# A linear-attention layer and a GELU MLP on one core: the state sums of four chunks accumulated in PSUM, and the second group's units planned ahead of the weights

## The chip, the cores and the metric

The kernel runs on 1 core of one Trainium2 chip. The time is the device time of one execution, in microseconds (us); before the change it is 546.49 us, the median of 3 runs (546.25 to 547.72). A core has TensorE (PE, matrix products), VectorE (DVE), ScalarE (ACT), GpSimd (POOL), and SyncE (SP), which here issues most transfers. Each engine works through its own list of instructions in order, and they wait for each other by semaphores. TensorE writes its results to PSUM, in banks, and VectorE and ScalarE read them there.

## The reference

```python
def _attn_ref(q, k, v, alpha):                # batch 4, heads 8, seq 768, head_dim 48
    state = np.zeros((B, H, D, D))
    for t in range(S):
        state = alpha[:, :, t, :, None] * state + np.einsum('bhd,bhe->bhde', k[:, :, t], v[:, :, t])
        y[:, :, t] = np.einsum('bhd,bhde->bhe', q[:, :, t], state)
    return y

def _moe_ref(x, w_in, w_out):                 # x 3072x384, w_in 384x2048, w_out 2048x384, float64 weights
    h = x @ w_in
    g = 0.5 * h * (1.0 + erf(h / sqrt(2)))
    return g @ w_out
```

A recurrence with a decay per channel gives y; y, with its heads laid side by side, goes through a two-layer MLP with an exact GELU.

## The kernel before

**Units.** The sequence of each batch is cut into 3 groups of 256 steps, so there are 12 groups (g = 0 to 11), and a group's 8 heads are two units of four heads (u = 0, 1): 24 units, numbered 2g + u. A unit has four chunks of 64 steps (j = 0 to 3). For a unit VectorE makes running products of the decay forward (`forward`, L251) and backward (`backward`, L262) and scales q and k with them. So within a unit the state is a plain sum of k v over the chunks, with no decay left between them.

A unit then passes TensorE three times. `scores` and `turned` (L281, L290) make the products of q and k within each chunk and a transposed k; ScalarE copies the latter (`turned_out`, L297) and VectorE masks the former (`masked`, L302). `inside` multiplies the masked scores with v (L319) and, chunk by chunk, k with v (L337): the state sum of each chunk, each in its own columns of the PSUM tile `ybank`. `chain` (L354, L356) turns these into the states ahead of chunks 1 to 3 and behind chunk 3 by four VectorE instructions, each of which adds one chunk's sum to the state before. `outside_part` (L381) multiplies q with those states and adds to the same `ybank`. `carry` (L361) rescales the last state for the next group of the same batch. Then `x_high` and `x_low` (L423, L427) split y into two parts, and after unit u = 1 `spread` (L436) moves six pieces of 16 rows so that x fills 128 partitions. A check of the decay's range on ScalarE (L162) decides at the end whether a general path has to redo the work; with these inputs it does not run.

**MLP.** Each f32 product is made from parts of high and low precision: `gemm1` (L444) is 18 matmuls for a slice f of 256 hidden features (f = 0 to 7) and one group, `gelus` (L455, L456) and `gelu_low` (L461) make the two parts of the GELU, `gemm2` (L472) is 12 matmuls into an accumulator. I call the two products of one (g, f) a step: 96 steps.

**Weights.** They arrive as 64-bit numbers in 16 pieces (a to p), two for a slice f. Each is fetched by SP and turned into a high and a low part by five VectorE instructions (L198, L202, L212, L217, L227), two ScalarE ones and one more on VectorE (L233).

**What sets the order.** A planner in the program places the operations of all engines by their costs (`COST`), their dependences and a rank; the result is written out in that order by hand and fixed for TensorE, VectorE, ScalarE and SP. `ORDER` gives the ranks of the first units (digits) and of the pieces (letters). A step (g, f) needs slice f's pieces and group g's x; until all pieces are there only groups 0 to 2 may have steps. Some buffers are single: the masked scores, the transposed k and the PSUM tiles `s` and `ybank`, so one unit's `inside` waits for the unit before.

**Tile shapes.** A matmul on 64 rows and 64 columns of operands takes a quarter of TensorE's array, and the program gives each its shape and place in it: L281, L319, L337 and L381 have 64x64 (rows x columns), L290, L444 and L472 128x128.

**Start.** `pads` (L104, L106) fills rows of the operand buffers that no load writes.

Of the kernel before, what the change touches and what calls it, by code (L numbers as in the profile page):

```python
# [8 lines left out]
F32 = mybir.dt.float32  # L9
# [6 lines left out]
ALU = mybir.AluOpType  # L16
# [7 lines left out]
WAIT = 0.15  # L24
SLOW = 1.8
COST = dict(
    scan=2.25, back=2.05, q=1.35, scores=1.2, kn=0.6, mask=0.62, inside=1.2, chain=1.15, outer=0.85, carry=0.26,
    xh=0.6, xl=0.65, spread=2.0, check=0.95, load=2.6, fetch=0.4, u=0.92, c0=0.56, c1=0.9, c2=0.56, c3=0.95, c4=0.92,
    hi=0.84, lo=0.9, gemm1=2.12, gelu=0.58, low=0.63, gemm2=2.1, part=1.1,
)  # L30
ORDER = "0 1 a b c d 2 e 3 f g 4 h i 5 j k l m n o p"


@with_exitstack
def gla_then_gelu_ffn(ctx: ExitStack, tc: tile.TileContext, q, k, v, alpha, qg, kg, ag, w_in, w_out, out):
    nc = tc.nc
    B, H, D, S = q.shape
    NF, P, NK, _ = w_in.shape
    DM, DFF = NK * P, NF * P
    NT = B * S  # L40
    C = 128
    G = 2 * C
    CS = C // 2
    NCH = G // CS
    DP = 64
    NPAIR = H // 2
    NU = NPAIR // 2
    DR = DP - D
    NF2 = NF // 2
    GPB = S // G  # L50
# [6 lines left out]
    const = ctx.enter_context(tc.tile_pool(name="const", bufs=1))  # L57
# [41 lines left out]
    def pads(i, n, p0, p1, eng):  # L99
        for r0 in (DP // 2, DP + DP // 2):  # L100
            r = slice(r0, r0 + DP // 2)
            t = data[i][n][r, p0:p1].rearrange("p a t -> p (a t)")
            if eng is nc.scalar:
                eng.copy(t, (ones if n == "a" else zero)[r].to_broadcast(t.shape))  # L104
            else:
                eng.memset(t, 1.0 if n == "a" else 0.0)  # L106

    for n in "akq":
        pads(0, n, 0, 1, nc.vector)
    for n, eng in (("a", nc.gpsimd), ("k", nc.scalar), ("q", nc.vector)):  # L110
        pads(0, n, 1, NPAIR, eng)
    for n, eng in (("a", nc.gpsimd), ("k", nc.scalar), ("q", nc.gpsimd)):
        pads(1, n, 0, NPAIR, eng)
    for t in vbuf:
        nc.gpsimd.memset(t[:, :, H * D :], 0.0)

    states = []
    for u in range(NU):
        states.append([const.tile([P, 2, D], F32, name=f"state{u}_{i}") for i in range(NCH + 1)])

    mask = const.tile([P, CS], F32, name="mask")
    nc.gpsimd.memset(mask, 1.0)
    for half in range(2):
        r = slice(half * CS, (half + 1) * CS)
        nc.gpsimd.affine_select(
            out=mask[r],
# [8 lines left out]
    ybank = ps_y.tile([P, 2, BANK], F32, name="ybank")  # L135
# [133 lines left out]
    def ends_batch(g, j):  # L269
        return g % GPB == GPB - 1 and j == NCH - 1  # L270
# [38 lines left out]
    def inside(g, u):  # L309
        d = cur[g, u]  # L310
        vn = vbuf[g % NB]
        for i in range(2):
            for j in range(NCH):
                c, b = j // 2, j % 2
                r, t = slice(b * CS, (b + 1) * CS), (2 * i + c) * CS
                for h in range(2):
                    o = slice(h * DP, (h + 1) * DP)
                    e = (4 * u + 2 * i + h) * D
                    nc.tensor.matmul(  # L319
                        ybank[o, b, t : t + CS],  # L320
                        lhsT=vn[r, c, e : e + DP],
                        rhs=d["ss"][r, h, 2 * i + c, :],
                        start=(i == 0 and c == 0),
                        stop=(j == 0 and g % GPB == 0),
                        skip_group_check=True,
                    )
        for j in range(NCH):
            if ends_batch(g, j):
                continue
            c, b = j // 2, j % 2  # L330
            r = slice(b * CS, (b + 1) * CS)
            for i in range(2):
                t = 2 * C + (2 * i + c) * D
                for h in range(2):
                    o = slice(h * DP, (h + 1) * DP)
                    e = (4 * u + 2 * i + h) * D
                    nc.tensor.matmul(  # L337
                        ybank[o, b, t : t + D],
                        lhsT=d["kn"][r, i, c * P + h * DP : c * P + (h + 1) * DP],
                        rhs=vn[r, c, e : e + D],  # L340
                        start=False,
                        stop=True,
                        skip_group_check=True,
                    )

    def chain(g, u):
        d = cur[g, u]
        st = states[u]
        for j in range(NCH):
            if ends_batch(g, j):  # L350
                continue
            new = ybank[:, j % 2, 2 * C : 2 * C + 4 * D].rearrange("p (i c d) -> p i c d", i=2, c=2)[:, :, j // 2]
            if g % GPB == 0 and j == 0:
                d["chain"] = nc.vector.tensor_copy(st[1], new)  # L354
            else:
                d["chain"] = nc.vector.tensor_tensor(out=st[j + 1], in0=new, in1=st[j], op=ALU.add)  # L356

    def carry(g, u):
        if ends_batch(g, NCH - 1):
# [240 lines left out]
    ranks = {}  # L600
    for i, name in enumerate(ORDER.split()):
        ranks[int(name) if name.isdigit() else ord(name) - ord("a")] = i
        if not name.isdigit():
            ranks["w", ord(name) - ord("a")] = i
    unit_rank = [ORDER.split().index(str(n)) if str(n) in ORDER.split() else 100.0 + n for n in range(n_units)]
    piece_rank = [ORDER.split().index(chr(ord("a") + n)) for n in range(2 * NF2)]

# [9 lines left out]
    def plan_unit(n):  # L617
# [18 lines left out]
        d["kn"] = op("ACT", "kn", lambda: turned_out(g, u), [d["scores"], p.get("inside")], rank=-1)  # L636
        d["mask"] = op("DVE", "mask", lambda: masked(g, u), [d["scores"], p.get("inside")], rank=-1)
        d["inside"] = op("PE", "inside", lambda: inside(g, u), [d["mask"], d["kn"], p.get("xh"), p.get("xl"), p.get("chain"), p.get("outer")], rank=r)
        for side in range(2):
            d["c%d" % side] = op("ACT", "check", lambda side=side: range_check(g, u, side), [d["mask"]], rank=200 + n)  # L640
        d["chain"] = op("DVE", "chain", lambda: chain(g, u), [d["inside"], pp_.get("carry")], rank=-1)
        d["outer"] = op("PE", "outer", lambda: outside_part(g, u), [d["chain"]], rank=r)
        if g < NSB:
# [45 lines left out]
    low_of, state = {}, {"g": None, "run": 0, "evac": None}  # L689
# [86 lines left out]
    def choose(e, t):  # L776
        best = None
        for o in waiting[e]:
            at = when(o)
            if at is not None and at <= t + 1e-9 and (best is None or (o.rank, o.n) < (best.rank, best.n)):  # L780
                best = o
        if e != "PE":
            return best
        if best is not None:
            return best
        second = [s for s in steps if s["gemm2"].start is None]
        if second:
            at = when(second[0]["gemm2"])
            if at is not None and at <= t + 1e-9:
                return second[0]["gemm2"]  # L790
        if len(second) < 2:
            hp_free = steps[-2]["low"].end if len(steps) > 1 else 0.0
            if hp_free is not None and hp_free + WAIT <= t + 1e-9 or len(steps) < 2:
                g = next_step(t)
                if g is not None:
                    return gemm1_op(g, t)
        return None

    t = 0.0
    idle = 0  # L800
    while True:
        moved = False
        for e in ("DVE", "ACT", "PE", "SP", "POOL"):
            if free_at[e] <= t + 1e-9:
                o = choose(e, t)
# [89 lines left out]
```

## Time and profile before

| what | us |
|---|---|
| median of 3 runs | 546.49 |
| the profiled execution | 546.99 |
| its span | 545.4 |
| TensorE matmul busy | 508.4 |
| VectorE busy | 306.5 |
| ScalarE busy | 201.3 |
| first matrix product of the MLP starts | 36.94 |
| last conversion instruction (L233) starts | 146.24 |

The profile is of one execution; times in it count from the start of its span. In the page's slices a digit is a tenth of busy time in one of 40 equal parts (13.6 us each), and in the row PEclk a tenth of TensorE's full clock. In a timeline, a row is: start, duration, engine, line, operation, output<-input, rows*columns of the operand in the array, shape, count. An f32 matmul shows as two rows, so x32 of L337 are 16 matmuls. The ends of matmuls are modelled, so starts are what I compare.

### The profile page before, as it was taken

How to read it: one execution, taken by the hardware profiler on the slowest of the kernel's cores; microseconds unless marked ns; L12 is line 12 of the kernel's file. 1: busy time of each engine (PE TensorE's matmuls, PEld its weight loads, DVE VectorE, ACT ScalarE, POOL GpSimd, SP SyncE). 2: the span in 40 equal slices, each digit the busy share in tenths (PEclk: the TensorE clock that was granted, in tenths of full speed). 3: DMA queues.
4: the chain of work that ended last, by engine and by line, in shares of the span. 5: the costliest groups of instructions: out<-in, count | busy, mean ns of one | idle time of the engine just before them, and what ended most of it. 6: DMA issues, size and time to landing. Idle time of an engine off the chain costs nothing.

```text
span 545.4 us, 13878 instructions
## 1 busy us (share of the span) xinstructions
PE 508.4 (93%) x5966; PEld 492.0 (90%) x5966; DVE 306.5 (56%) x573; ACT 201.3 (37%) x387; POOL 38.9 (7%) x51
## 2 busy tenths in 40 slices
PE   6547588999999999999999999999999999999996
PEld 6436588999999999999999999999999999999995
DVE  7999989999997878666337345142231221211211
ACT  3625345554443444433243243243223222222221
POOL 5000000000012121111001000000000000000000
PEclk9559589999999999999999999999999999999998
DMA  6974344533014344405005002001000000000001
GB/s 196 298 216 136 114 117 160 143 119 103 0 32 132 103 133 121 130 2 161 2 1 162 1 6 85 1 1 46 1 32 14 1 30 1 16 14 1 30 0 34
DMA packets 20723, 39.49 MB, mean 72 GB/s; under 512 B 4113, under 2 KB 7617, under 8 KB 20657
## 3 DMA queue, kind: packets, MB, share of 16 engines
q1 hardware_dynamic: 19136, 33.93, 20.7%
q0 software_dynamic: 1232, 4.33, 2.3%
q8 instruction: 49, 0.80, 0.6%
q10 hardware_dynamic: 288, 0.30, 0.2%
q14 instruction: 18, 0.14, 0.1%
HBM read 31.46 MB, written 4.72 MB: 66 GB/s over the span
## 4 chain that ended last, share of the span: by engine, by line
PE 84%; DVE 9%; DMA 2%; issue 2%; ACT 1%; ACTq 0%; DVEq 0%; SPq 0%
PE hp L444 37%; PE acc L472 35%; PE ybank L381 4%; PE s L290 2%; PE ybank L319 2%; PE s L281 2%; PE ybank L337 2%; DVE rp L262 1%; DVE st L217 1%; DVE pp L251 1%; DMA ad<-in_ag_dram 1%; DMA x<-z 1%; DVE w L202 1%; DVE state L356 1%; DVE w L227 1%
## 5 line engine op out<-in xcount | busy, mean ns | idle before, releaser
L444 PE MATMUL hp<-x,wih 128*128 128x256 f32 x1152 | 215.5, 287 | 7.6 <-DMA x<-z 7.6
L444 PEld LDWEIGHTS hp<-x,wih 128*128 128x128 f32 x1152 | 184.5, 193 | 8.9 <-ACT wih L230 7.8
L461 DVE TENSOR_TENSOR glo<-hp,ghi 128x512 fp32r<-128x512 f32 x96 | 66.1, 689 | 185.0 <-ACT hp L456 183.8
L444 PE MATMUL hp<-x,wil 128*128 128x256 f32 x576 | 163.9, 285 | 0.0
L455 ACT ACTIVATE ghi<-hp 128x512 fp32r<-128x512 f32 x96 | 57.5, 599 | 247.4 <-PE hp L444 247.3
L472 PE MATMUL acc<-woh,ghi 128*128 128x384 f32 x384 | 131.6, 343 | 1.4 <-ACT ghi L455 1.4
L472 PE MATMUL acc<-wol,ghi 128*128 128x384 f32 x384 | 128.6, 335 | 0.0
L444 PEld LDWEIGHTS hp<-x,wil 128*128 128x128 f32 x576 | 111.3, 193 | 0.0
L472 PE MATMUL acc<-woh,glo 128*128 128x384 f32 x384 | 82.2, 335 | 1.8 <-DVE glo L461 1.8
L472 PEld LDWEIGHTS acc<-woh,ghi 128*128 128x128 f32 x384 | 72.4, 188 | 2.6 <-ACT ghi L455 1.8
L472 PEld LDWEIGHTS acc<-wol,ghi 128*128 128x128 f32 x384 | 72.4, 189 | 0.0
L472 PEld LDWEIGHTS acc<-woh,glo 128*128 128x128 f32 x384 | 67.9, 188 | 2.2 <-DVE glo L461 2.2
L456 ACT ACTIVATE hp<-hp 128x512 f32<-128x512 f32 x96 | 57.1, 595 | 0.0
L258 POOL TENSOR_TENSOR qd<-qd,pp 128x512 f32<-128x512 f32 x18 | 23.2, 1287 | 226.0 <-DVE pe L252 158.3
L262 DVE TENSOR_TENSOR_SCAN rp<-ad,rp,top 128x255 f32<-128x255 f32 x48 | 35.3, 776 | 0.1
L381 PEld LDWEIGHTS ybank<-qd,state 48*48 48x48 f32 x704 | 23.7, 131 | 10.4 <-DVE state L356 6.6
L356 DVE TENSOR_TENSOR state<-ybank,state 128x96 f32<-128x96 f32 x80 | 20.5, 257 | 21.2 <-PE ybank L337 19.0
L381 PE MATMUL ybank<-qd,state 48*48 48x64 f32 x704 | 27.6, 233 | 5.3 <-DVE state L356 5.2
L251 DVE TENSOR_TENSOR_SCAN pp<-ad,top 128x256 f32<-128x256 f32 x48 | 30.4, 674 | 0.5 <-DMA ad<-in_ag_dram 0.5
L319 PEld LDWEIGHTS ybank<-ss,vn 64*64 64x64 f32 x768 | 14.5, 144 | 13.2 <-DVE ss L302 6.7
L319 PE MATMUL ybank<-ss,vn 64*64 64x64 f32 x768 | 18.0, 236 | 8.5 <-DVE ss L302 5.5
L496 POOL DMA_DIRECT2D out_dram<-part x11 | 8.3, 753 | 243.8 <-DVE part L490 164.6
(63 smaller groups left out, 397.0 us busy)
## 6 DMA issues: line engine op xcount, KB each, us to landing
st<-in_moe_w_in_dram SPq DMA_DIRECT2D x8, 768.0 KB, 4.8
st<-in_moe_w_out_dram SPq DMA_DIRECT2D x8, 768.0 KB, 4.8
ad<-in_ag_dram SPq DMA_DIRECT2D x48, 96.0 KB, 2.3
kd<-in_kg_dram SPq DMA_DIRECT2D x48, 96.0 KB, 2.3
qd<-in_qg_dram SPq DMA_DIRECT2D x48, 96.0 KB, 2.4
vn<-in_v_dram SPq DMA_DIRECT2D x12, 384.0 KB, 3.9
out_dram<-part POOLq DMA_DIRECT2D x11, 384.0 KB, 3.7
x<-z SPq DMA_DIRECT2D x63, 32.0 KB, 2.9
```

Of the source, the lines that this page charges most:

```text
L251: nc.vector.tensor_tensor_scan(pp[:, i], at[:, i], top, MID, ALU.mult, ALU.min)
L258: nc.gpsimd.tensor_tensor(out=qt, in0=qt, in1=pp, op=ALU.mult)
L262: nc.vector.tensor_tensor_scan(rp[:, i, G - 2 :: -1], at[:, i, G - 1 : 0 : -1], top[:, 1:], rp[:, i, G - 1 :], ALU.mult, ALU.min)
L281: nc.tensor.matmul(d["s"][o, h, e : e + CS], lhsT=d["kt"][r, i, t], rhs=d["qt"][r, i, t], start=True, stop=True)
L319: nc.tensor.matmul(ybank[o, b, t : t + CS], lhsT=vn[r, c, e : e + DP], rhs=d["ss"][r, h, 2 * i + c, :], start=(i == 0 and c == 0), stop=(j ...
L356: d["chain"] = nc.vector.tensor_tensor(out=st[j + 1], in0=new, in1=st[j], op=ALU.add)
L381: ins = nc.tensor.matmul(ybank[r, b, t : t + CS], lhsT=states[u][j][r, i], rhs=d["qt"][r, i, j * CS : (j + 1) * CS], start=False, stop=Tru ...
L444: nc.tensor.matmul(hp[:, j, :], lhsT=a[:, j, i * P : (i + 1) * P], rhs=x[:, i, :], start=(i == 0 and n == 0), stop=(i == NK - 1 and n == 2),)
L455: nc.scalar.activation(ghi, hp, AF.Gelu)
L456: nc.scalar.activation(hp, hp, AF.Gelu)
L461: nc.vector.tensor_tensor(out=glo, in0=hp, in1=ghi.bitcast(F32), op=ALU.subtract)
L472: nc.tensor.matmul(acc[t], lhsT=a[:, j, t * C : (t + 1) * C], rhs=w[:, j, :], start=(first and j == 0 and k == 0 and w is wo_hi[f]), stop= ...
```

## The change

`inside` no longer leaves each chunk's own sum but, for chunk j, the sum over all chunks up to j: TensorE accumulates it in PSUM. Chunks 0 and 1 lie in the first 128 steps, chunks 2 and 3 in the second; for chunk 1 the two are taken as one matmul over 128 rows, for chunk 2 a 128-row matmul of the first half and a 64-row one, for chunk 3 two 128-row ones. So a unit has 24 such matmuls in place of 16, and also where a batch ends, where the last chunk's sum was left out (12 before). Their columns in `ybank` are reordered, so that `chain` is one VectorE instruction of 128x384 that adds the state ahead of the unit to all four (a copy in a batch's first group). The five states of a unit's heads lie in one tile, `held`.

The planner's cost of `chain` goes from 1.15 to 0.5, and `ORDER` puts units 2 and 3 ahead of piece a, and units 4 and 5 behind f and g. The pads of the first two head pairs are VectorE's; q's others go to ScalarE.

```diff
-    scan=2.25, back=2.05, q=1.35, scores=1.2, kn=0.6, mask=0.62, inside=1.2, chain=1.15, outer=0.85, carry=0.26,
+    scan=2.25, back=2.05, q=1.35, scores=1.2, kn=0.6, mask=0.62, inside=1.2, chain=0.5, outer=0.85, carry=0.26,
...
-ORDER = "0 1 a b c d 2 e 3 f g 4 h i 5 j k l m n o p"
+ORDER = "0 1 2 3 a b c d e f 4 5 g h i j k l m n o p"
...
     for n in "akq":
-        pads(0, n, 0, 1, nc.vector)
-    for n, eng in (("a", nc.gpsimd), ("k", nc.scalar), ("q", nc.vector)):
-        pads(0, n, 1, NPAIR, eng)
+        pads(0, n, 0, 2, nc.vector)
+    for n, eng in (("a", nc.gpsimd), ("k", nc.scalar), ("q", nc.scalar)):
+        pads(0, n, 2, NPAIR, eng)
...
-    states = []
-    for u in range(NU):
-        states.append([const.tile([P, 2, D], F32, name=f"state{u}_{i}") for i in range(NCH + 1)])
+    held = [const.tile([P, NCH + 1, 2 * D], F32, name=f"state{u}") for u in range(NU)]
+    states = [[t[:, j].rearrange("p (i d) -> p i d", i=2) for j in range(NCH + 1)] for t in held]
...
         for j in range(NCH):
-            if ends_batch(g, j):
-                continue
-            c, b = j // 2, j % 2
-            r = slice(b * CS, (b + 1) * CS)
+            b = j % 2
             for i in range(2):
-                t = 2 * C + (2 * i + c) * D
+                t = 2 * C + (2 * (j // 2) + i) * D
                 for h in range(2):
                     o = slice(h * DP, (h + 1) * DP)
                     e = (4 * u + 2 * i + h) * D
-                    nc.tensor.matmul(
-                        ybank[o, b, t : t + D],
-                        lhsT=d["kn"][r, i, c * P + h * DP : c * P + (h + 1) * DP],
-                        rhs=vn[r, c, e : e + D],
-                        start=False,
-                        stop=True,
-                        skip_group_check=True,
-                    )
+                    for c in range(j // 2 + 1):
+                        r = slice(0, P if c < j // 2 or b else CS)
+                        nc.tensor.matmul(
+                            ybank[o, b, t : t + D],
+                            lhsT=d["kn"][r, i, c * P + h * DP : c * P + (h + 1) * DP],
+                            rhs=vn[r, c, e : e + D],
+                            start=False,
+                            stop=True,
+                            skip_group_check=True,
+                        )
...
     def chain(g, u):
         d = cur[g, u]
-        st = states[u]
-        for j in range(NCH):
-            if ends_batch(g, j):
-                continue
-            new = ybank[:, j % 2, 2 * C : 2 * C + 4 * D].rearrange("p (i c d) -> p i c d", i=2, c=2)[:, :, j // 2]
-            if g % GPB == 0 and j == 0:
-                d["chain"] = nc.vector.tensor_copy(st[1], new)
-            else:
-                d["chain"] = nc.vector.tensor_tensor(out=st[j + 1], in0=new, in1=st[j], op=ALU.add)
+        new = ybank[:, :, 2 * C : 2 * C + 4 * D].rearrange("p b (c e) -> p b c e", c=2)
+        to = held[u][:, 1:].rearrange("p (c b) e -> p b c e", b=2)
+        if g % GPB == 0:
+            d["chain"] = nc.vector.tensor_copy(to, new)
+        else:
+            old = held[u][:, 0].unsqueeze(1).unsqueeze(1).to_broadcast([P, 2, 2, 2 * D])
+            d["chain"] = nc.vector.tensor_tensor(out=to, in0=new, in1=old, op=ALU.add)
```

The order that the planner makes of it moves on TensorE ahead of the first matrix product (L444 before, L440 now; a name ends in a buffer's number; `s` are scores, `ss` masked scores, `kn` the transposed k). Before, from unit 0's inner part to the first matmuls of unit 1's outer part:

```order
L319 MATMUL ybank<-ss_0_277,vn_115 64x64 x16
L337 MATMUL ybank<-vn_115,kn_0_275 64x48 x16
L281 MATMUL s_1_320<-qd_118,kd_117 64x64 x16
L290 MATMUL s_1_320<-ident,kd_117 128x128 x4
L381 MATMUL ybank<-qd_118,state_1_144 48x64 x4
```

Now, from the same place to the first matrix product:

```order
L318 MATMUL ybank<-ss_0_267,vn_115 64x64 x16
L335 MATMUL ybank<-vn_115,kn_0_265 64x48 x24
L280 MATMUL s_1_326<-qd_118,kd_117 64x64 x16
L289 MATMUL s_1_326<-ident,kd_117 128x128 x4
L377 MATMUL ybank<-qd_118,state_143 48x64 x12
L280 MATMUL s_0_374<-qd_122,kd_121 64x64 x16
L289 MATMUL s_0_374<-ident,kd_121 128x128 x4
L318 MATMUL ybank<-ss_1_350,vn_115 64x64 x16
L335 MATMUL ybank<-vn_115,kn_1_348 64x48 x24
```

Units 2 and 3 (buffers `qd_122`, `kd_121`) now pass between units 0 and 1 and the first matrix product, and the state sums have 24 matmuls.

On VectorE, behind unit 1's scans and unit 0's mask, before (`u`, `w`, `st`: a weight piece's buffers):

```order
L302 TENSOR_TENSOR ss_0_277<-s_0_249,mask 128x512
L198 TENSOR_SCALAR u_270<-u_270 128x768
L202 SCALAR_TENSOR_TENSOR w_314<-st_211,u_270 128x768
L212 TENSOR_SCALAR u_270<-w_314 128x768
L217 SCALAR_TENSOR_TENSOR st_211<-st_211,u_270 128x768
L354 COPY state_1_144<-ybank 128x96
L356 TENSOR_TENSOR state_2_145<-ybank,state_1_144 128x96
L356 TENSOR_TENSOR state_3_146<-ybank,state_2_145 128x96
L356 TENSOR_TENSOR state_4_147<-ybank,state_3_146 128x96
```

and now:

```order
L301 TENSOR_TENSOR ss_0_267<-s_0_235,mask 128x512
L250 SCALAR_TENSOR_TENSOR pp_0_269<-ad_120,top 128x256 x2
L251 TENSOR_SCALAR pe_0_271<-pp_0_269 128x2
L252 RECIPROCAL rp_0_270<-pe_0_271 128x2
L254 TENSOR_TENSOR qd_122<-qd_122,pp_0_269 128x512
L261 SCALAR_TENSOR_TENSOR rp_0_270<-ad_120,rp_0_270,top 128x255 x2
L264 TENSOR_TENSOR kd_121<-kd_121,rp_0_270 128x512
L349 COPY state_143<-ybank 128x2x2x96
L301 TENSOR_TENSOR ss_1_350<-s_1_326,mask 128x512
```

Unit 2's scans stand where the first piece's conversion stood; unit 3's follow, and the first piece comes behind them. SP's list changes with it: the loads of units 2 and 3 now come ahead of the first three weight fetches.

## The prediction

> **What bounds the kernel now.** I read the page first: its busy line, its 40 slices and the clock row.
>
> ```profile
> span 545.4 us, 13878 instructions
> PE 508.4 (93%) x5966; PEld 492.0 (90%) x5966; DVE 306.5 (56%) x573; ACT 201.3 (37%) x387; POOL 38.9 (7%) x51
> PE   6547588999999999999999999999999999999996
> DVE  7999989999997878666337345142231221211211
> PEclk9559589999999999999999999999999999999998
> ```
>
> TensorE is the bound from about slice 7 (95 us) on. Before that VectorE is full and TensorE waits, half of the time at half clock. The view by stretches of time (us, then PE busy, PEld, DVE, ACT, POOL, clock, DMA share, GB/s) makes it sharp:
>
> ```profile
> 110.00:130.00 20.00, 20.00 (x242) 19.17 (x241) 19.21 (x32) 9.85 (x18) 0.00 (x0) 1.00 0.41 126
> 200.00:300.00 100.00, 100.00 (x1485) 96.14 (x1484) 61.38 (x128) 38.63 (x85) 11.85 (x11) 1.00 0.28 81
> ```
>
> So there are two stages. In the first, whatever brings TensorE to its steady work sooner moves the end. In the second nothing waits that could be shortened: every nanosecond added on TensorE is added to the end, and VectorE time saved there is worth nothing. 18 of the 24 units (groups 3 to 11) run in the second.
>
> **TensorE's added work.** The timeline of TensorE in the second stage, around one unit's inner part and state sums:
>
> ```profile
> 170.11 0.40 PE L444 MATMUL hp<-x,wih 128*128 128x256 f32 x2
> 170.35 0.28 PE L444 MATMUL hp<-x,wil 128*128 128x256 f32 x1
> 170.56 0.69 PE L319 MATMUL ybank<-ss,vn 64*64 64x64 f32 x32
> 171.07 0.68 PE L337 MATMUL ybank<-vn,kn 64*64 64x48 f32 x32
> 171.69 0.44 PE L472 MATMUL acc<-woh,ghi 128*128 128x384 f32 x1
> ...
> 186.37 0.62 PE L337 MATMUL ybank<-vn,kn 64*64 64x48 f32 x24
> 186.92 0.44 PE L472 MATMUL acc<-woh,ghi 128*128 128x384 f32 x1
> ```
>
> An f32 matmul stands as two rows, so 16 matmuls of L337 take 171.07 to 171.69, 0.62 us; the 12 of a batch's last unit 0.55. The change makes them 24 in every unit: 4 on 64 rows x 64 columns of the array for chunk 0, 4 on 128x64 for chunk 1, eight that take turns 128x64, 64x64 for chunk 2, eight on 128x64 for chunk 3. Counted along the list, the shape changes 9 times: once behind chunk 0, seven times within chunk 2, once ahead of chunk 3.
>
> What does a change of shape cost? In the rows above two L444 matmuls take 170.11 to 170.35, 0.12 each from start to start, but from the last of them (170.35) to the first 64x64 row (170.56) it is 0.21: 0.09 more. The same shows where only the columns change, from 128 to 1:
>
> ```profile
> 401.66 0.28 PE L444 MATMUL hp<-x,wil 128*128 128x256 f32 x1
> 401.87 0.19 PE L832 MATMUL tp<-ones,total 128*1 128x1 f32 x2
> ```
>
> Again 0.21. No row of before changes the rows alone, which is what the new list does; by these neighbours I price it at 0.09 too, and keep nothing as the lower end. The Trainium skill's page TensorEngine Tiling (Array Packing), Key Properties, says that changing the tiling mode, and not just the tile, drains TensorE, and its list of configurations has 128x64 and 64x64 as different modes. By that rule the group takes the 2.03 us below, without it 1.05; the trace agrees with it at each change that it has.
>
> The price of one small matmul has two neighbours, L337 and this:
>
> ```profile
> 102.95 1.10 PE L381 MATMUL ybank<-qd,state 48*48 48x64 f32 x32
> 103.98 0.50 PE L444 MATMUL hp<-x,wih 128*128 128x256 f32 x2
> ```
>
> With one change of shape at the end taken off, L337 gives (0.62 - 0.09)/16 = 0.033 and L381 (1.03 - 0.09)/16 = 0.059. A matmul that a change follows overlaps with nothing, 0.059 + 0.09 = 0.15; the other 15 I put at 0.04, since half of them have a neighbour in the other half of the columns. Group: 9 x 0.15 + 15 x 0.04 + 0.09 at the exit = 2.03. Added per unit: 1.41, and 1.48 in the 6 of the 18 units that had 12 matmuls. Second stage: 12 x 1.41 + 6 x 1.48 = **25.8 us**. Lowest with changes (0.123 and 0.033): 1.70, so 1.08 a unit; highest (0.15 and 0.059): 2.32, so 1.70 a unit; 20 to 31 us.
>
> **VectorE's addition.** Four additions become one of 128x384. Rows: the four of a unit, and an addition of the new size out of PSUM (grouped view: busy, mean ns).
>
> ```profile
> 52.84 1.12 DVE L356 TENSOR_TENSOR state<-ybank,state 128x96 f32<-128x96 f32 x4
> 53.88 0.95 DVE L233 TENSOR_TENSOR wil<-w,wih 128x768 fp32r<-128x768 f32 x1
> 54.74 1.38 DVE L262 TENSOR_TENSOR_SCAN rp<-ad,rp,top 128x255 f32<-128x255 f32 x2
> ...
> L486 DVE TENSOR_TENSOR part<-part,acc 128x384 f32<-128x384 f32 x10 | 5.0, 547 | 0.5 <-PE acc L472 0.5
> ```
>
> From 52.84 to 53.88 is 1.04; the new one is 0.5, the least I allow, and 1.04 the most if its cut-up pattern costs what four did. So 0.5 saved in each of six early units, 3 us of VectorE, counted in the walk below; in the other 18 units TensorE hides it.
>
> **Pads and loads.** Six VectorE memsets of 512 columns stand ahead of the first scan.
>
> ```profile
> L106 DVE MEMSET qd<- 32x768 f32 x2 | 1.4, 698 | 0.4 <-issue 0.4
> 5.53 1.27 DVE L251 TENSOR_TENSOR_SCAN pp<-ad,top 128x256 f32<-128x256 f32 x2 [0.52 <-DMA ad<-in_ag_dram]
> ```
>
> At no more than 0.70 each they end by 1.05 + 4.2 = 5.3, and that scan waits for its load until 5.53: nothing, or some tenths either way where a q load waits for its pad. Group 1's loads pass the first three weight fetches on SP; the first piece is now wanted only at 27.6 by the walk below, which is the cover. Were it gone, a fetch that lands late would stop VectorE by as much.
>
> **The first stage, walked along VectorE's and TensorE's new order.** Steps from start to start in these rows (scans of a unit, mask, five conversion steps of a piece), and TensorE at half and at full clock:
>
> ```profile
> 10.06 1.27 DVE L251 TENSOR_TENSOR_SCAN pp<-ad,top 128x256 f32<-128x256 f32 x2
> 13.67 0.69 DVE L265 TENSOR_TENSOR kd<-kd,rp 128x512 f32<-128x512 f32 x1
> 15.05 0.69 DVE L302 TENSOR_TENSOR ss<-s,mask 128x512 f32<-128x512 f32 x1 [0.69 <-ACT kn L297]
> 15.66 0.55 DVE L198 TENSOR_SCALAR u<-u 128x768 int32<-128x768 int32 x1
> 37.44 0.56 DVE L198 TENSOR_SCALAR u<-u 128x768 int32<-128x768 int32 x1
> 40.61 0.96 DVE L227 TENSOR_TENSOR w<-w,st 128x768 f32<-128x768 f32 x1
> ...
> 16.71 1.10 PE L337 MATMUL ybank<-vn,kn 64*64 64x48 f32 x32
> 17.54 1.15 PE L281 MATMUL s<-qd,kd 48*64 48x64 f32 x32
> ...
> 36.94 3.95 PE hp L444 x18
> 529.40 2.15 PE hp L444 x18
> 533.64 2.15 PE hp L444 x18
> ```
>
> A unit's scans take 4.2 (10.06 to 13.67 + 0.61), a mask 0.61, a piece 4.9 (4.07 for five steps, 0.87 for L233), one step of both matrix products 4.24 (529.40 to 533.64). At half clock L337 takes 0.83 against 0.53 without its exit, so the new group there is 2.03 x 0.83/0.53 = 3.2.
>
> VectorE is free from 14.3, as before. Up to unit 3's addition it has two units' scans (8.4), 2.8 pieces (13.7), three additions (1.5), four masks (2.4) and some 3 us of carries, low parts and the first gelu: 29.1. It waits four times, 6.2 in all: 2.2 ahead of unit 1's mask (unit 0's group ends at 19.1, unit 1's scores and copy at 21.9), 0.7 at unit 2's addition, 0.7 at the first gelu, 2.6 at unit 3's addition, because its group runs at half clock behind the first matrix product (41.4 to 45.4) until 49.5. Behind that addition stands the third weight piece, for which TensorE waits. So 49.6. From there to unit 5's addition: 4.6 pieces 22.5, two units 8.4, three additions 1.5, a dozen others at 0.6 (five gelus, two masks, partial sums, low parts) 7.5, waits 1.6: 91.1. Unit 5's outer part ends 1.0 later, at 92.2, with six steps done. Before, that point is 103.98 with seven steps and half of the eighth, 1.5 x 4.24 = 6.4 of work more: 97.6 for the same work. **Lead: 5.4 us.** Without changes of shape the group takes about 1.05 (1.7 at half clock), the waits shrink from 7.8 to about 2.6, and the lead is 10.6. From there two groups' steps lie ready for TensorE, so I add no wait.
>
> **Sum.** 545.4 + 25.8 - 5.4 = 565.8 of span. The profiled execution took 546.99, 1.6 more than its span, and the median of the runs is 0.5 below it: **567 us**. Its own range, from 20 to 31 added and a lead of 0 to 10.6: 557 to 577.
>
> **The rivals.** *No price for a change of rows alone*: the 0.09 belongs to the columns or to the full array. 24 matmuls at 0.04 and the exit make 1.05, 0.43 a unit; 18 x 0.43 + 0.4 = 8.1, minus the lead of 10.6: 544, and 541 to 552 for 0.033 to 0.059 a matmul. For it: no row shows such a change; against it: each change that rows do show costs the same 0.09, the columns-only one too. It ends on the other side, faster, as long as a unit gains less than 0.57 (10.6/18). *A change also bares the weight load*:
>
> ```profile
> L337 PEld LDWEIGHTS ybank<-vn,kn 64*64 64x64 f32 x704 | 15.5, 146 | 0.0
> ```
>
> Loads of 0.146 are hidden now. If each change bares one instead of 0.09, it is 9 x 0.056 = 0.5 more a unit, 9 us: 576, up to 590 with the dear matmul. Against it: the 0.09 was measured with a load behind it. *The addition saves nothing* (it costs as four did): 3 us of lead less, inside the ranges.
>
> **How the numbers follow.** Chances: forecast 0.60, no price 0.28, bared load 0.12. Within 0.3% (1.6 us, about what a measurement here can tell from no change) are 544.9 to 548.1: of the middle case 0.17 lie below, 0.07 within, 0.04 above. Faster 0.17, same 0.07, slower 0.76. The range 543 to 578 holds nearly all of the forecast (0.58), most of the middle case (0.18) and the bottom of the last (0.04): 0.8. The forecast's own is 557 to 577.
>
> **What would show it.** Right: the state-sum group at about 2 us in the second stage, its rows 0.15 apart in chunk 2; TensorE still 100 of 100 us between 200 and 300, with the steps between units unchanged; the outer part of unit 5 over near 92. Wrong: that group near 1 us, or TensorE waiting in the second stage; a first matrix product before 38, or one after 45 with the clock at 0.50 beyond 60, would break the walk.

## The result, and the profile after

The changed kernel took **602.19 us** (median of 4 runs, 601.3 to 603.13) against 546.85 us (546.25 to 547.72) for the kernel before on the same chip: a ratio of 1.101, 95% interval 1.0987 to 1.1035. The forecast was slower, 567 us, with a range of 543 to 578. The direction was right; the time lies 35 us over the forecast and 24 over the range.

The page of the profiled execution after (602.54 us): the span, the busy line, and the slices of TensorE, VectorE and the clock (a slice is 15.0 us now).

```profile
span 600.9 us, 14720 instructions
PE 574.7 (96%) x6414; PEld 546.3 (91%) x6414; DVE 305.9 (51%) x513; ACT 201.7 (34%) x389; POOL 38.5 (6%) x51
PE   5899599899999999999999999999999999999996
DVE  8767899997996765756623713513213111121211
PEclk8557799899999999999999999999999999999999
```

TensorE is busy for 66.3 us more than before and idle for 10.8 less (26.2 against 37.0); VectorE's total has hardly moved (306.5 to 305.9). So the four additions that became one are paid for on the engine that is the bound. Where TensorE's time went stands in the grouped view (busy us, mean ns; L335 is L337 of before, L352 is L356):

```profile
L335 PE MATMUL ybank<-vn,kn 128*64 128x48 f32 x768 | 56.2, 241 | 0.0
L335 PE MATMUL ybank<-vn,kn 64*64 64x48 f32 x384 | 41.5, 236 | 0.0
L352 DVE TENSOR_TENSOR state<-ybank,state 128x384 f32<-128x384 f32 x16 | 8.9, 557 | 51.4 <-PE ybank L335 51.4
```

The new addition costs 0.56, as forecast (0.5). It waits 51 us for L335 over the execution, which is harmless in the second stage. The timeline of TensorE, around the state sums of one unit at half clock and of one at full clock (starts are what counts):

```profile
15.63 5.11 PE L335 MATMUL ybank<-vn,kn 64*64 64x48 f32 x48
20.67 1.13 PE L280 MATMUL s<-qd,kd 48*64 48x64 f32 x32
...
214.64 3.20 PE L335 MATMUL ybank<-vn,kn 64*64 64x48 f32 x48
217.78 0.44 PE L468 MATMUL acc<-woh,ghi 128*128 128x384 f32 x1
```

From the group's first start to the next line's: **3.14 us** at full clock, 5.04 at half. Before it was 0.62 and 0.83; the forecast said 2.03 and 3.2. The group is one row in the timeline, since L335 follows L335. The view of one line's instructions inside a short stretch opens it up (duration in ns: least, median, most; first and last start; shapes). Here are chunk 2's eight matmuls, which take turns in shape, and chunk 3's eight, which don't, in the unit whose group runs from 273.47 to 276.60:

```profile
L335 PE MATMUL ybank<-vn,kn x16: 218/222/257, 274.1 to 275.8; 128*64 128x48 f32 x8, 64*64 64x48 f32 x8
...
L335 PE MATMUL ybank<-vn,kn x16: 222/222/257, 276.0 to 276.4; 128*64 128x48 f32 x16
```

Chunk 2 starts at 274.1 and chunk 3 at 276.0: eight matmuls in 1.9 us, 0.24 each. Chunk 3's sixteen rows start within 0.4 us, some 0.06 a matmul. No row is slower by itself (222 ns in both); the time is in the distance between starts.

The view by stretches (us, PE busy, PEld, DVE, ACT, POOL, clock, DMA share, GB/s) shows the two stages:

```profile
15.00:35.00 20.00, 17.36 (x256) 14.49 (x252) 12.86 (x24) 4.20 (x9) 0.00 (x0) 0.50 0.51 177
35.00:55.00 20.00, 18.31 (x256) 15.90 (x254) 15.05 (x23) 11.97 (x22) 0.00 (x0) 0.56 0.65 179
...
110.00:130.00 20.00, 20.00 (x159) 19.68 (x159) 19.09 (x28) 10.39 (x18) 0.00 (x0) 0.91 0.42 144
200.00:300.00 100.00, 100.00 (x1543) 91.95 (x1542) 62.56 (x116) 34.81 (x79) 13.71 (x12) 1.00 0.31 90
```

The second stage is as forecast: TensorE 100 of 100 us, nothing waits that could be shortened, and 18 longer groups go straight to the end. The first stage is not. The same two early stretches of the kernel before:

```profile
15.00:35.00 20.00, 9.00 (x212) 7.89 (x212) 19.40 (x37) 8.19 (x17) 0.00 (x0) 0.50 0.97 277
35.00:55.00 20.00, 14.50 (x180) 13.07 (x182) 18.11 (x30) 10.14 (x16) 0.00 (x0) 0.84 0.44 144
```

VectorE, the engine that was full there, was busy 37.5 of 40 us before and 27.9 after. What it waits for, in its timeline between 15 and 57 us (the wait and its releaser in brackets):

```profile
20.77 0.56 DVE L349 COPY state<-ybank 128x384 f32<-128x384 f32 x1 [1.89 <-PE ybank L335]
23.50 0.69 DVE L301 TENSOR_TENSOR ss<-s,mask 128x512 f32<-128x512 f32 x1 [2.17 <-ACT kn L296]
35.28 0.56 DVE L349 COPY state<-ybank 128x384 f32<-128x384 f32 x1 [3.06 <-PE ybank L335]
45.76 0.56 DVE L352 TENSOR_TENSOR state<-ybank,state 128x384 f32<-128x384 f32 x1 [2.79 <-PE ybank L335]
...
56.17 0.56 DVE L352 TENSOR_TENSOR state<-ybank,state 128x384 f32<-128x384 f32 x1 [1.87 <-PE ybank L335]
```

Four of these five are the state sums themselves: the chain is planned at 0.5, but stands on VectorE behind a group that takes 5 us at half clock (the last of the four behind one of 3.1 at full clock).

### The profile page after: what moved, and what is told of

It reads as the page before. It is cut to its first block, busy times and chain, and to the rows that moved or that the text cites. A ratio compares the mean times of both kernels' runs of the same rounds, so it can differ in the third digit from the quotient of the medians.

```text
span 600.9 us, 14720 instructions
## 1 busy us (share of the span) xinstructions
PE 574.7 (96%) x6414; PEld 546.3 (91%) x6414; DVE 305.9 (51%) x513; ACT 201.7 (34%) x389; POOL 38.5 (6%) x51
## 4 chain that ended last, share of the span: by engine, by line
PE 87%; DMA 4%; DVE 4%; ACT 2%; issue 1%; SPq 1%; POOL 0%; ACTq 0%; DVEq 0%; POOLq 0%
PE hp L440 34%; PE acc L468 32%; PE ybank L335 12%; PE ybank L377 3%; PE ybank L318 3%; PE s L289 2%; PE s L280 2%; DMA ad<-in_ag_dram 1%; DMA st<-in_moe_w_in_dram 1%; DMA x<-z 1%; DMA vn<-in_v_dram 1%; SPq L149 1%; ACT kd L104 1%; DVE w L201 0%; DVE rp L261 0%
## 5 line engine op out<-in xcount | busy, mean ns | idle before, releaser
L440 PE MATMUL hp<-x,wih 128*128 128x256 f32 x1152 | 216.2, 287 | 6.3 <-DMA x<-z 6.3
L440 PEld LDWEIGHTS hp<-x,wih 128*128 128x128 f32 x1152 | 184.9, 193 | 7.6 <-issue 6.4
L440 PE MATMUL hp<-x,wil 128*128 128x256 f32 x576 | 164.3, 285 | 0.0
L440 PEld LDWEIGHTS hp<-x,wil 128*128 128x128 f32 x576 | 111.6, 194 | 0.0
L335 PE MATMUL ybank<-vn,kn 128*64 128x48 f32 (+1 forms) x1152 | 82.6, 239 | 0.0
L335 PEld LDWEIGHTS ybank<-vn,kn 128*64 128x64 f32 (+1 forms) x1152 | 68.3, 145 | 12.7
L296 ACT COPY kn<-s 128x512 f32<-128x512 f32 x24 | 14.1, 587 | 90.9 <-PE ybank L335 79.4
L352 DVE TENSOR_TENSOR state<-ybank,state 128x384 f32<-128x384 f32 x16 | 8.9, 557 | 51.4 <-PE ybank L335 51.4
```

Source lines behind the costliest of these rows:

```text
L296: nc.scalar.copy(d["kn"], d["s"][:, :, 2 * C : 4 * C])
L335: nc.tensor.matmul(ybank[o, b, t : t + D], lhsT=d["kn"][r, i, c * P + h * DP : c * P + (h + 1) * DP], rhs=vn[r, c, e : e + D], start=False ...
L440: nc.tensor.matmul(hp[:, j, :], lhsT=a[:, j, i * P : (i + 1) * P], rhs=x[:, i, :], start=(i == 0 and n == 0), stop=(i == NK - 1 and n == 2),)
```

## The experiments

All ratios are to the kernel before on the same chip.

**1. One change of shape in place of nine.** The same 24 matmuls, put in order so that the 64-row ones come first:

```diff
+        def sums(j, c):                      # the matmuls of chunk j that read half c
+            ...
+        for j, c in ((0, 0), (2, 1), (1, 0), (2, 0), (3, 0), (3, 1)):
+            sums(j, c)
```

> The changed kernel with the same 24 state-sum matmuls of a unit in another order: first all on 64x64 (chunk 0, second half of chunk 2), then all on 128x64. One change of shape in place of nine. Theory S (each change of shape costs, and a matmul between two changes loses its overlap, 0.24 us): the group falls from 3.13 to 24 x 0.058 + 2 x 0.09 = 1.6 us; 18 units x 1.5 = 28 us less, and some 6 to 10 less in the first stage where the group takes 5.05: 564 to 570. Theory W (128-row matmuls are dear in themselves, order does not matter): group near 3.1, 602.

Measured: 569.31 us (566.56 to 570.2), ratio 1.039 [1.035, 1.043]. TensorE around a group (L334 is the state sums):

```profile
241.15 1.69 PE L334 MATMUL ybank<-vn,kn 64*64 64x48 f32 x48
242.76 0.51 PE L442 MATMUL hp<-x,wih 128*128 128x256 f32 x2
```

1.61 us with the same matmuls on the same data. So 33 of the 55 us were the order of the list, not its length: 27.2 of them in the second stage (the table below), where 18 x 1.52 = 27.4.

**2. Three changes, and five.** Three: chunks in their natural order, each half by itself. Five: chunk 2 in pairs for each pair of heads (two on 128x64, two on 64x64), so that no matmul stands alone between two changes. The edit of the first, against experiment 1's list:

```diff
-        for j, c in ((0, 0), (2, 1), (1, 0), (2, 0), (3, 0), (3, 1)):
+        for j, c in ((0, 0), (1, 0), (2, 0), (2, 1), (3, 0), (3, 1)):       # three
```

> The changed kernel with chunk 2's eight matmuls in two runs of four (128x64, then 64x64): three changes of shape in place of nine, the rest as it is. Theory S: group 24 x 0.058 + 4 x 0.09 = 1.75 us, so about 3 us above the grouped order in the second stage, 568 to 574. Theory W: 602. If changes cost but less than linearly, it lies near the grouped order.

> The changed kernel with the 24 matmuls of a unit put so that the array's shape changes five times and no matmul stands alone between two changes (chunk 2 in pairs for each pair of heads: two on 128x64, two on 64x64). The group took 1.62 us with one change and 1.88 with three. Theory L (what costs most is the lone matmul between two changes, a change beside a pair costs 0.13): 1.88 + 2 x 0.13 = 2.14, so 573.6 + 18 x 0.26 = 578 of time, 576 to 580. Theory C (every change costs the same 0.19, (3.13 - 1.62)/8): 1.62 + 4 x 0.19 = 2.38, so 573.6 + 18 x 0.50 = 582.6, 581 to 586.

Measured: three 573.61 us (570.96 to 575.86), 1.0495 [1.0448, 1.0541]; five 581.28 us (579.61 to 581.82), 1.0615 [1.0581, 1.0648]. The group with three changes, then with five:

```profile
252.91 1.96 PE L334 MATMUL ybank<-vn,kn 64*64 64x48 f32 x48
254.79 0.44 PE L470 MATMUL acc<-woh,ghi 128*128 128x384 f32 x1
```

```profile
261.65 2.22 PE L335 MATMUL ybank<-vn,kn 64*64 64x48 f32 x48
263.80 0.45 PE L474 MATMUL acc<-woh,ghi 128*128 128x384 f32 x1
```

1.88 and 2.15: each change beside a pair costs 0.13, as theory L had it; theory C's 2.38 is out. What a lone matmul loses can be read from starts inside the groups, in narrow windows of the timeline: in the changed kernel one matmul (two rows) on 64x64 and the next, and in the five-change kernel a pair (four rows) on 64x64 and the next pair:

```profile
274.75 0.31 PE L335 MATMUL ybank<-vn,kn 64*64 64x48 f32 x2
274.99 0.32 PE L335 MATMUL ybank<-vn,kn 128*64 128x48 f32 x2
```

```profile
262.45 0.32 PE L335 MATMUL ybank<-vn,kn 64*64 64x48 f32 x4
262.70 0.32 PE L335 MATMUL ybank<-vn,kn 128*64 128x48 f32 x4
```

The lone matmul takes 0.24 us and the pair 0.25: the second of a pair, on the other 64 columns of the array, runs beside the first at hardly any cost. That chunk 2's matmuls add two by two to the same columns of `ybank` is not the reason, since chunk 3's do so too, at 0.06 each.

The time of the five-change kernel, 581.3, nevertheless fell on C's side. The group's 2.15 shows that it isn't C: the excess arose before the second stage. The state sums of unit 6, the first of the second stage, mark the border:

| kernel | changes in a group | group us | unit 6's group starts | span less that |
|---|---|---|---|---|
| new order and pads alone | 0 | 0.61 | 124.99 | 422.2 |
| one change | 1 | 1.61 | 128.50 | 439.4 |
| three | 3 | 1.88 | 124.91 | 444.4 |
| five | 5 | 2.15 | 131.26 | 448.9 |
| the change itself | 9 | 3.13 | 134.29 | 466.6 |

From row to row the last column grows by 18 times the group: 18 x 0.27 = 4.9 against 5.0, 4.9 against 4.5, 18 x 0.98 = 17.6 against 17.7. Only from the first row to the second it is 1.2 less than the groups say (18.4 against 17.2). The fourth column scatters by several us and not in the order of the groups: the first stage is a tangle of waits that falls differently each time.

**3. The order and the pads alone** (16 matmuls and four additions as before; the pads as the change has them):

```diff
-ORDER = "0 1 a b c d 2 e 3 f g 4 h i 5 j k l m n o p"
+ORDER = "0 1 2 3 a b c d e f 4 5 g h i j k l m n o p"
...
```

> The kernel before with the new ORDER and pads alone: 16 state-sum matmuls and four additions as before. Theory S: nothing added in the second stage, and the new order leads in the first stage by some 6 to 9 us (10.6 of the walk less what four additions cost more and the waits): 537 to 541. Rival O (the order itself loses, because the first matrix product comes later and the clock stays at half): 548 to 556.

Measured: 548.15 us (10 runs), 1.002 [1.0003, 1.0036]. There was no lead to be had even without the long groups. The first stretches of that kernel, and then its engines around the second group's x:

```profile
15.00:35.00 20.00, 11.05 (x262) 9.66 (x258) 15.78 (x34) 6.38 (x14) 0.00 (x0) 0.50 0.50 176
35.00:55.00 20.00, 16.42 (x270) 14.88 (x264) 16.72 (x32) 10.73 (x20) 0.00 (x0) 0.66 0.70 214
```

```profile
56.75 0.91 ACT L194 ACTIVATE u<-st 128x768 f32<-128x768 f32 x1 [2.78 <-DVE st L217]
56.81 1.95 ACTq L436 DMA_DIRECT2D x<-z  x3
60.17 0.77 PE L444 MATMUL hp<-x,wih 128*128 128x256 f32 x2 [4.57 <-DMA x<-z]
```

VectorE is busy 32.5 of the 40 us against 37.5 before: with four units in a row there is nothing to convert between their waits on TensorE at half clock. The new order takes 5.0 us of VectorE's time in the very stretch where it was to gain some. TensorE then waits 4.57 us for the second group's x.

**4. The sums alone** (before's ORDER and pads, the rest of the change as it is):

```diff
-ORDER = "0 1 2 3 a b c d e f 4 5 g h i j k l m n o p"
+ORDER = "0 1 a b c d 2 e 3 f g 4 h i 5 j k l m n o p"
...
```

> The changed kernel with the ORDER and pads of before: state sums in PSUM and one addition alone. Theory S: 18 x 2.5 = 45 us in the second stage and 8 to 12 in the first, where four groups at half clock take 4.2 more each on the way to the first matrix products: 600 to 606. If the new order is worth 6 to 9 us also with the long group, this is 608 to 611; rival O: 590 to 596.

Measured: 600.94 us (600.3 to 601.49), 1.0984 [1.0956, 1.1011], with the same groups of 3.13 and 5.04. The sums alone make nearly the whole loss; with either form of the sums, order and pads move the time by 0.2%.

**5. Which half of the order.** Units 2 and 3 early but 4 and 5 where they were (with the new pads), and the reverse (with the pads of before):

```diff
+ORDER = "0 1 2 3 a b c d e f g 4 h i 5 j k l m n o p"      # units 2 and 3 early
+ORDER = "0 1 a b c d 2 e 3 f 4 5 g h i j k l m n o p"      # units 4 and 5 early
```

> The kernel before with the new pads and half of the new ORDER: units 2 and 3 ahead of piece a, units 4 and 5 where they stood before (4 behind g, 5 behind i). The whole new order with pads gave 548.2, 1.3 over before. Theory A (putting units 2 and 3 first costs, since the first three weight pieces come later and TensorE's first matrix product with them, and the second group's x is late anyway): 548 to 550. Theory B (the loss comes from units 4 and 5 behind f and g; units 2 and 3 early would gain the lead that the prediction gave them): 541 to 546.

> The kernel before with the other half of the new ORDER: units 2 and 3 where they stood before, units 4 and 5 ahead of g; pads of before. Theory A (units 2 and 3 are what costs): 545 to 547, the same as before or a little under it. Theory B (units 4 and 5 are what costs): 548 to 550.

Measured: 555.3 us (550.61 to 556.36), 1.0115 [1.0076, 1.0154], and 549.55 us (546.83 to 550.87), 1.0032 [1.0014, 1.0049]. Neither half gains, and neither theory holds as written: A forecast no loss for the second (549.55 lies in B's range), B a gain for the first, whose 555.3 lies above both ranges. Their parts don't add up to the whole (1.002). With units 2 and 3 early and 5 late, TensorE runs dry where it was full before: it waits for VectorE three times between 97 and 110 us (1.82, 2.62 and 1.27 us), where the kernel before has it busy for 14 of 14 us from 96 to 110. What the planner does with the ranks in between is not settled by these runs.

**6. A transfer on ScalarE's queue.** After unit 5, the changed kernel shows ScalarE's queue held by three issues, a GELU behind them, and TensorE behind the GELU:

```profile
104.00 5.02 ACTq L432 DMA_DIRECT2D x<-z  x3
109.06 0.60 ACT L451 ACTIVATE ghi<-hp 128x512 fp32r<-128x512 f32 x1 [5.74 <-DMA ad<-in_ag_dram]
...
109.71 0.44 PE L468 MATMUL acc<-woh,ghi 128*128 128x384 f32 x1 [2.61 <-ACT ghi L451]
```

TensorE stands idle for 2.61 us and falls to half clock behind it (the 0.91 between 110 and 130 above). I took this for 4.6 us of the loss. The edit, on the changed kernel and on the order alone:

```diff
-                eng = nc.scalar if h and g < NSB else nc.sync
+                eng = nc.gpsimd if h and g < NSB else nc.sync
```

> The changed kernel with ScalarE's half of the x spread (L432, groups 0 to 2) issued from GpSimd's queue, so that no GELU stands behind a transfer that cannot be issued. Theory Q (the 5.0 us that ScalarE spent issuing three transfers at 104.0 held the GELU and cost TensorE about 4.6 us): the GELU's wait of 5.74 is gone and the time is 597 to 599. Rival (TensorE would wait there for x or another weight piece anyway): 601 to 604, with TensorE still idle for some 3 us between 100 and 115.

> The kernel before with the new order and pads (548.2), and ScalarE's half of the x spread (L436, groups 0 to 2) on GpSimd's queue, where no weight conversion stands ahead of it (at 56.8 it stood behind one that had waited 2.8 us for VectorE). Theory Q (the second group's x, for which TensorE waited 4.6 us at 60.2, was late by that queue): the wait shrinks to 3.7 or less and the time to 545 to 547. Rival (VectorE's three conversion steps ahead of the x parts, and the other half on SP, make it late anyway): 547.5 to 549, the wait still over 4 us.

Measured: on the changed kernel 604.64 us (603.14 to 605.55), 1.1044 [1.1009, 1.1079]; on the order alone 547.55 us, 0.9987 [0.9972, 1.0003]. On the changed kernel the theory fell. The GELU's wait shrank to 1.66, and TensorE waited a few us later instead:

```profile
106.56 0.60 ACT L451 ACTIVATE ghi<-hp 128x512 fp32r<-128x512 f32 x1 [1.66 <-PE hp L440]
...
111.62 0.96 PE L468 MATMUL acc<-woh,glo 128*128 128x384 f32 x4 [1.54 <-DVE glo L457]
113.88 0.48 PE L440 MATMUL hp<-x,wih 128*128 128x256 f32 x2 [1.30 <-DMA x<-z]
```

From unit 5's group to unit 6's it is 38.2 us with the stall (96.1 to 134.3) and 38.6 without (97.7 to 136.3). The stall was real and on the chain of waits, and worth nothing, because the next wait stood right behind it. On the order alone, TensorE's wait for x grew from 4.57 to 6.65 us in the profiled execution, as the rival had it; but that execution, at 550.86 us, was the slowest of the twelve, so the wait says little of the median. The time is not told apart from the kernel before.

**7. The one addition only where VectorE was full.** The accumulated sums, in the order with one change, in groups 0 and 1; separate sums and four additions in all others:

```diff
+NSUM = 2
...
+        if g >= NSUM:      # in inside and in chain: as before; below it: the accumulated sums, one instruction
+            ...
```

> The accumulated sums and their one VectorE instruction only in groups 0 and 1 (units 0 to 3, one change of shape), the kernel before's separate sums in the other 20 units, with the order and pads of before. It keeps 4 x 0.5 = 2 us of VectorE's saving where VectorE is full and leaves the second stage untouched. Theory V (VectorE's time in the first stage moves the start of the steady work): 544.5 to 545.5. Theory N (TensorE's longer groups there, 2.8 us at half clock against 1.1, and the other waits take it back): 546.5 to 549.

> As the kernel with early sums in groups 0 and 1 alone, but with the new order and pads. Theory V: order and pads alone gave 548.2, so 2 us of VectorE saved make it 546, 545 to 547. Theory N: 548 to 551, since units 2 and 3, which now run ahead of the first matrix product at half clock, each wait for the longer group.

Measured: with the old order 547.07 us (12 runs), 1.0003 [0.999, 1.0017]; with the new one 548.67 us, 1.0033 [1.0012, 1.0053]. This leaves the second stage alone and keeps the saving, and it is worth nothing: theory N. VectorE's waits in the first 35 us with the old order:

```profile
15.26 0.69 DVE L302 TENSOR_TENSOR ss<-s,mask 128x512 f32<-128x512 f32 x1 [0.92 <-ACT kn L297]
19.88 0.56 DVE L384 COPY state<-ybank 128x384 f32<-128x384 f32 x1 [0.88 <-PE ybank L356]
22.59 0.69 DVE L302 TENSOR_TENSOR ss<-s,mask 128x512 f32<-128x512 f32 x1 [1.29 <-ACT kn L297]
30.18 0.56 DVE L384 COPY state<-ybank 128x384 f32<-128x384 f32 x1 [1.47 <-PE ybank L356]
```

4.6 us, where the kernel before shows a single wait of 0.69: the 2 us saved go into such waits, two of them for the longer groups. None of these versions beats the kernel before. In all of them, and in the change itself, the planner's cost of `inside` stayed at 1.2; a list planned with the cost of the longer group was not tried.

## Why the prediction was wrong in size

**What held.** Two stages, with TensorE saturated in the second, so that the added matmul time goes to the end one for one: the table's last column shows it to within 1.2 us in 17. A change of rows alone costs, so the rival "no price for a change of rows alone", which held 0.28 of the chance, was wrong. The Trainium skill's page TensorEngine Tiling (Array Packing), Key Properties, has a change of tiling mode drain TensorE; the runs fit that (0.13 us for each change of rows between 64 and 128), and the page has no figure. The new addition was right (0.56 against 0.5), and so was the rest of the second stage.

The whole difference, split at unit 6's group, with the order-and-pads kernel between (the group and what follows, first that kernel, then the changed one):

```profile
124.99 0.68 PE L337 MATMUL ybank<-vn,kn 64*64 64x48 f32 x32
125.60 0.50 PE L444 MATMUL hp<-x,wih 128*128 128x256 f32 x2
```

```profile
134.29 3.20 PE L335 MATMUL ybank<-vn,kn 64*64 64x48 f32 x48
137.42 0.50 PE L440 MATMUL hp<-x,wih 128*128 128x256 f32 x2
```

| part | forecast | measured | from |
|---|---|---|---|
| second stage | +25.8 | +44.4 | 466.6 less 422.2 |
| first stage, the sums | | +9.3 | 134.29 less 124.99 |
| order and pads, whole span | | +1.8 | spans 547.2 less 545.4 |
| the lead (the two rows above) | -5.4 | +11.1 | |
| span | +20.4 | +55.5 | 600.9 less 545.4 |

**The first failed step: the price of a group, 2.03 in place of 3.13.** It gives 18.6 of the 35 us missed. Two terms of that sum were mis-sized. (a) *A matmul that a change follows: 0.15 forecast, 0.24 measured in chunk 2*; eight of them make 0.7 of the 1.1. The 0.09 came from rows where a change was followed by a long run of the new shape, and it priced only the wait ahead of the new shape. With one, three and five changes the whole price is 0.13, and where a single matmul stands between two changes another 0.06 goes: nine changes at 0.13, 24 matmuls at 0.058 and the exit of 0.09 make 2.65, and 3.13 - 2.65 = 0.48 over eight matmuls is 0.06. That is the place of the neighbour that a lone matmul lacks: alone it takes as long as a pair (experiment 2). (b) *A matmul without a change: 0.04 forecast, 0.058 measured*: the one-change group less its change, (1.61 - 0.13 - 0.09)/24. A quarter-array matmul before had three other quarters to run beside; the new ones have one neighbour, the 64-row ones too, since the list puts them all on rows 0 to 63. I gave the new ones almost the old price. The rival with a bared weight load, 2.5 a group, was nearer than the forecast, and its 0.146 for a change is nearer to the measured 0.13 than 0.09 is (its upper end, by its own terms, is 577 + 9 = 586 and not 590). The traces bear out a part of it: the load behind a change starts with its matmul (both rows at 274.50 in the changed kernel), while inside a run it starts 0.04 ahead of it (241.50 and 241.54 in experiment 1). Whether the 0.13 is the load left bare or the array running empty, these runs do not tell apart.

**The second failed step: the lead of 5.4.** It became a lag of 11.1, 16.5 us away, in two places of the walk. (a) *The waits counted up to unit 5.* The walk took each unit's work on VectorE as work that could be moved forward, with 6.2 us of waits up to unit 3's addition. That addition came at 56.17 in place of 49.6: the five waits shown above make 11.8 us, since the half-clock group took 5.04 and not 3.2. Behind it TensorE waited 6.27 us (until 68.05) for the second group's x, and unit 5's outer part was over at 102.5 in place of 92.2, with the six steps done that the walk had: 10.3 of the 16.5. (b) *"I add no wait" behind that point.* TensorE waited 2.61 us at 109.71 and fell to half clock, where the kernel before has it busy for 14 of 14 us from 96 to 110. These, and what comes behind them, are the other 6.2.

The order alone, with short groups, leads nowhere either, where the walk had 10.6. It counted some 2.6 us of waits; VectorE waited 6.5 us up to 50 us in that kernel (3.70, 0.83 and 2.01), since the weight pieces that were taken out from between the first units were what had filled its waits. TensorE's first matrix product moved from 36.94 to 44.17 (to 48.25 in the changed one; forecast 41.4), and the clock returned to full later with it. At 91.5, with unit 5's outer part over, that kernel was still some 4 us ahead (an estimate with the walk's 4.24 a step). A wait of 2.25 us at 101.82, for VectorE's `glo`, and the half clock behind it (0.72 from 101.8 to 108) took that: by 112.5 us it had started just as many rows of the two products, the state sums and the outer parts as the kernel before (180, 108, 176 and 176 in both). So its lead was nought, and its 1.8 us arose later. What the changed kernel would gain with any one of these waits gone is open: moving one transfer only showed that another wait stood behind it.

**The range.** Its upper end, 578, allowed no lag in the first stage, and 31 us in the second, with at most 0.15 for a lone matmul, a bound from rows with only one change in them. Both gave way. The only matmul of the profile of before that stands alone between two changes is this one, with a single column (TensorE's timeline):

```profile
401.87 0.19 PE L832 MATMUL tp<-ones,total 128*1 128x1 f32 x2
401.99 0.69 PE L319 MATMUL ybank<-ss,vn 64*64 64x64 f32 x32
```

0.12 from start to start, close to the sum's lower bound of 0.123; but it streams one column where the new ones stream 48, and with no other row for it the bound should have been wider.

## What to carry to other kernels

Order matmuls so that those of the same shape stand together, and next to a neighbour on the other part of the array: the same 24 matmuls took 1.61 us with one change of rows and 3.13 with nine, and in a kernel that TensorE bounds this is paid one for one (27 us in the second stage here, 33 in all). Before moving work from an idle engine to the one that is the bound, ask what a microsecond saved is worth: here VectorE's saving was worth nothing in both stages, in the second because TensorE hid it, in the first because VectorE went on to wait, for TensorE among others. And a wait on the chain is worth no more than the gap to the next one.

## What the runs showed of the hardware

*A change of rows between 64 and 128 has a price, and a lone matmul pays twice*: 0.13 us for the change, and between two changes a single f32 matmul takes 0.24 us, as long as a pair on the two halves of the columns (0.25), in place of 0.058 inside a run, at full clock.

*Work on parts of the array went with half clock.* Three stretches of the changed kernel: units 1 to 3 ahead of the first matrix product (48.25), the product's first 4 us, and what follows.

```profile
30.00:48.00 18.00, 16.31 (x234) 13.83 (x228) 11.63 (x19) 6.42 (x13) 0.00 (x0) 0.50 0.43 115
48.20:52.30 4.10, 4.10 (x22) 3.91 (x18) 4.03 (x7) 2.85 (x6) 0.00 (x0) 0.50 0.99 306
52.60:54.00 1.40, 1.40 (x53) 1.24 (x49) 0.74 (x2) 1.40 (x3) 0.00 (x0) 1.00 0.05 15
```

TensorE is busy for 16.3 of 18 us, mostly with matmuls on 48 to 128 rows and 48 or 64 columns, and the clock stays at 0.50; some 4 us after the 128x128 products begin it is full. In the order-and-pads kernel they begin at 44.17 and the clock is 0.50 until 48.4 and 1.00 from 49.0. The Trainium skill's page TensorE: Matmul & The Clock Gate, Part 1, states that some 3.4 us of sustained work bring the clock back to full. The 4 us behind the large products fit; the 18 us before don't, and no run here shows whether it is the size of the tiles or the short gaps between them. In the second stage, groups of 3.13 us between large products left the clock at 1.00.
